# Seven-product weight sums of the second MLP formed in the streaming buffer, with the elementwise sums on VectorE

## The chip, the cores and the metric

The kernel runs on one core of one Trainium2 chip. The metric is the device time of one execution in microseconds (us). TensorE multiplies matrices, VectorE, ScalarE and GpSimd work elementwise, and SyncE (SP) issues nearly all transfers; each engine runs its own stream of instructions in order and waits for the others by semaphores.

## The reference

Three stages follow each other: a causal attention with a bias from cumulated gates (4 batches, 8 heads, 576 positions, head size 64), a first MLP with a softmax and a layer norm (512 to 1024 to 512), and the second MLP, which the change is in:

```
def _moe2_ref(x, w_in, w_out):        # x: 2304 x 512, w_in: 512 x 2048, w_out: 2048 x 512
    h = x @ w_in
    relu6 = np.clip(h + 3.0, 0.0, 6.0)
    g = h * relu6 / 6.0
    return (g @ w_out).astype(np.float32)
```

The weights come in 64-bit floats and are decoded on the chip. Each 32-bit factor is kept as a high and a low part, and each product is three matmuls: high by high, low by high, high by low.

## The kernel before

A planner (`Plan`, L51) sets the order. The functions call `plan.add(engine, cost, function, reads, writes, ...)`, and `emit` runs a greedy list schedule by the costs written there; what it gives is one fixed stream for each engine. `lag` is the planner's guess of how long a transfer takes to land, `new` names a ring of buffers, `bank` asks for one of eight PSUM banks.

The second MLP treats its 2304 tokens in groups of three tiles of 128 rows, so 384 tokens in one matmul. The hidden 2048 units are 16 blocks of 128 (`m`), or 8 pairs (`k`).

*The first six tiles* are two trios (`ci` 0 and 1), computed directly. For a trio and a block, `ffn2_h` does twelve matmuls (L1120: x parts `xk` by weight parts `wp`) into a bank; `gated` takes the bank through ScalarE (relu, L1097), VectorE (multiplication, L1100, tile `ggs`), ScalarE (high part, L1104) and VectorE (low part, L1107, tile `gs`); `ffn2_out` does nine matmuls (L1132: `gs` by `w2o`) into three accumulator banks. Trio 1 runs 3.5 blocks behind trio 0 (`DELAY`), and output matmuls come two items after their product (`LAG`). Beside these items the weights of the later blocks are decoded by `split64`: a raw load on SP (L321, L323; 512 KB each, in a ring of two buffers and one single buffer), ScalarE's shift (L329), VectorE's unit extraction (L333) and join (L337), the high part on ScalarE (L346), the low part on VectorE for the input weights and on GpSimd for the output weights (both L353).

*The last twelve tiles* are two batches (`bi`) of six tiles. For a pair of hidden blocks, a product of 2x2 blocks is done with seven block products in place of eight (`pair_h`: 42 matmuls, L1272, from x forms `xb` and weight forms `ws`; sums of the products `c` on VectorE, L1285), then four gates and 36 output matmuls. Six banks hold the six tiles' accumulators. The x forms come from `load_x2_pair`: four loads `xs` (L1205) into the places of trio 0's x parts, the split on ScalarE (L1212) and VectorE (L1215), and four differences `less` on GpSimd (L1218).

*The weight forms* are made ahead, beside the first six tiles, and kept in DRAM (`ws_d`). For a pair, `pair_parts` stores three pieces of the decoded weights as they are (L1153, L1157; 256 KB each). `pair_sums` makes a full sum of the weights' two parts (L1166, 1024 elements a partition), four sums of quarters (L1171 to L1174), a high part on ScalarE (L1178), a low part on VectorE (L1181), and stores both (L1184; 512 KB each). The sums of pairs 0 to 3 are on GpSimd, those of pairs 4 to 7 on VectorE (`SUMS_DVE`). `load_pair` then loads all seven forms of a pair in one transfer of 1792 KB (L1248) into a ring of two buffers, for either batch; these buffers take the place that the raw buffers had.

## Time and profile before

| | us |
|---|---|
| median of three runs (844.49 to 845.88) | 844.82 |
| the profiled execution, whole | 844.44 |
| its span, first to last instruction | 842.6 |
| TensorE busy | 805.1 |
| VectorE busy | 544.1 |
| ScalarE busy | 422.6 |
| GpSimd busy | 254.6 |

The granted TensorE clock was 0.994 of full speed over the span. The second MLP's direct six tiles lie at about 445 to 585 us, the two batches of six tiles behind them to the end. Busy times are sums over stages of different kinds; a timeline of one engine gives for each group of instructions its start, its length, and in brackets how long the engine idled before it and what ended that.

### The profile page before, as it was taken

What the parts mean: (1) busy time and instruction counts of PE and PEld (TensorE: products, weight loads), DVE (VectorE), ACT (ScalarE), POOL (GpSimd) and SP (SyncE); (2) the same over time, 40 slices, a digit from 0 to 9 for tenths busy, and PEclk for the clock granted to TensorE, in tenths of its full rate; (3) what the DMA queues carried; (4) which work ended last, traced back from release to release, by engine and by line L of the source; (5) the groups of instructions that cost most, each with busy time, mean ns of one, the idle gap of its engine ahead of it and who ended that gap; (6) DMA issues with size and microseconds to landing.
All of it is one profiled execution on the core that took longest, in us unless ns stands there. A gap on an engine that the chain in (4) does not pass through costs nothing.

```text
span 842.6 us, 14160 instructions
## 1 busy us (share of the span) xinstructions
PE 805.1 (96%) x4960; PEld 698.2 (83%) x4960; DVE 544.1 (65%) x1300; ACT 422.6 (50%) x986; POOL 254.6 (30%) x336
## 2 busy tenths in 40 slices
PE   3889999999999999999999988998999999999998
PEld 2655588898898889888998977997999898898896
DVE  3687887746855574749727999767645457555451
ACT  2575768755765575737535564334423234423223
POOL 2464644424633363327305564004000000000000
PEclk9999999999999999999999999999999999999999
DMA  6753596755555455233505566968522422623302
GB/s 160 191 154 110 120 221 144 176 122 126 129 119 135 103 124 120 65 110 115 189 32 159 198 214 228 306 201 287 213 87 98 165 88 100 237 89 109 154 1 75
DMA packets 113670, 121.60 MB, mean 144 GB/s; under 512 B 65120, under 2 KB 95328, under 8 KB 111552
## 3 DMA queue, kind: packets, MB, share of 16 engines
q1 hardware_dynamic: 111296, 112.32, 46.4%
q10 hardware_dynamic: 2304, 8.39, 3.0%
q8 instruction: 39, 0.64, 0.3%
q14 instruction: 31, 0.25, 0.1%
HBM read 74.74 MB, written 24.71 MB: 118 GB/s over the span
## 4 chain that ended last, share of the span: by engine, by line
PE 80%; DVE 11%; DMA 4%; issue 2%; POOL 2%; ACT 1%; SPq 0%; DVEq 0%; POOLq 0%; ACTq 0%
PE bank L1132 19%; PE bank L1272 14%; PE bank L905 11%; PE bank L818 10%; PE bank L713 6%; PE bank L616 5%; PE bank L684 5%; PE bank L1120 4%; PE bank L589 3%; PE bank L884 2%; DVE gs L1107 2%; DVE wp L353 2%; PE bank L479 1%; DVE t_w2i L333 1%; DVE a_w2o L337 1%
## 5 line engine op out<-in xcount | busy, mean ns | idle before, releaser
L1132 PE MATMUL bank<-w2o,gb 128*128 128x512 f32 x576 | 136.4, 391 | 0.0
L1132 PEld LDWEIGHTS bank<-w2o,gb 128*128 128x128 f32 x576 | 107.7, 188 | 21.0
L1272 PE MATMUL bank<-xb,ws 128*128 128x384 f32 x672 | 122.7, 336 | 0.6 <-DVE c L1285 0.6
L1272 PEld LDWEIGHTS bank<-xb,ws 128*128 128x128 f32 x672 | 118.3, 188 | 3.5 <-DVE c L1285 1.0
L1285 DVE TENSOR_TENSOR c<-c,bank 128x384 f32<-128x384 f32 x112 | 60.3, 552 | 83.7 <-PE bank L1272 70.0
L537 DVE CUSTOM_DVE_ANT_0 y<-bank,mask 96x288 f32<-96x288 f32 (+4 forms) x168 | 74.6, 467 | 57.2 <-PE bank L616 38.2
L549 ACT ACTIVATE y<-y,nmax 128x256 f32<-128x256 f32 (+4 forms) x140 | 83.5, 598 | 40.7 <-DVE nmax L537 28.4
L632 POOL TENSOR_SCALAR y<-y,rsum 128x128 f32<-128x128 f32 (+4 forms) x120 | 68.3, 588 | 103.4 <-DVE rsum L628 42.6
L905 PE MATMUL bank<-zh,w_out_h 128*128 128x256 f32 x288 | 82.9, 288 | 0.0
L905 PE MATMUL bank<-zh,w_out_l 128*128 128x256 f32 x288 | 81.0, 281 | 0.0
L905 PE MATMUL bank<-zl,w_out_h 128*128 128x256 f32 x288 | 81.0, 281 | 0.0
L1120 PE MATMUL bank<-xk,wp 128*128 128x384 f32 x384 | 74.8, 343 | 6.2 <-DVE ggs L1100 4.2
L1132 PE MATMUL bank<-w2o,gs 128*128 128x512 f32 x288 | 74.4, 403 | 3.6 <-DVE gs L1107 3.6
L1120 PEld LDWEIGHTS bank<-xk,wp 128*128 128x128 f32 x384 | 68.6, 191 | 11.1 <-DVE ggs L1100 6.2
L1132 PEld LDWEIGHTS bank<-w2o,gs 128*128 128x128 f32 x288 | 54.8, 193 | 14.7 <-DVE gs L1107 4.9
L1218 POOL TENSOR_TENSOR xs<-xs,xs 128x768 f32<-128x768 f32 x8 | 16.6, 2069 | 157.4 <-DVE xb L1215 112.6
L1097 ACT ACTIVATE ggb<-c 128x384 f32<-128x384 f32 x64 | 32.3, 522 | 58.2 <-DVE c L1285 57.6
L818 PE MATMUL bank<-w_in_h,xh 128*128 128x512 f32 x144 | 60.7, 421 | 0.8 <-DVE xh L800 0.8
L616 PE MATMUL bank<-stack 128*96 128x288 f32 (+4 forms) x288 | 57.9, 318 | 0.6 <-DMA stack<-rows_d 0.6
L818 PE MATMUL bank<-w_in_h,xl 128*128 128x512 f32 x144 | 56.8, 394 | 0.6 <-POOL xl L804 0.6
L818 PE MATMUL bank<-w_in_l,xh 128*128 128x512 f32 x144 | 56.7, 394 | 0.0
L905 PEld LDWEIGHTS bank<-zh,w_out_h 128*128 128x128 f32 x288 | 54.3, 189 | 1.1 <-DVE zl L891 0.2
(241 smaller groups left out, 1572.1 us busy)
## 6 DMA issues: line engine op xcount, KB each, us to landing
ws<-ws_d SPq DMA_DIRECT2D x16, 1792.0 KB
raw_w2i<-in_moe_w_in_dram SPq DMA_DIRECT2D x16, 512.0 KB
...
```

Of the source, the lines that this page charges most:

```text
L537: nc.vector.tensor_tensor_reduce(out=ys[h, t][:n, c0:c1], in0=bank(key)[:n, : c1 - c0], in1=mask[:n, 480 + n - w + c0 : 480 + n - w + c1], ...
L549: nc.scalar.activation(out=y[:n], in_=y[:n], func=AF.Exp, bias=nmax[:n, h, t : t + 1], scale=-1.0, accum_out=sums[:n, h, t : t + 1])
L616: nc.tensor.matmul(bank(key)[:n, : c1 - c0], lhsT=ss[:, 2 - 2 * m, ST[t] : w], rhs=ss[:, 3 - 2 * m, c0:c1], start=(m == 0), stop=(m == 1))
L632: nc.gpsimd.tensor_scalar(ys[h, t][:n], ys[h, t][:n], rsum[:n, h, t : t + 1], 1.0, ALU.mult, ALU.mult)
L684: nc.tensor.transpose(bank(key)[: SZ[jj], c : c + SZ[t]], ys[h, t][: SZ[t], ST[jj] : ST[jj] + SZ[jj]], ident[: SZ[t], : SZ[t]])
L713: nc.tensor.matmul(bank(key)[j * D : (j + 1) * D, lo - c0 : c1 - c0], lhsT=vs[v_key(p, a)][:n, jj, j, :], rhs=pts[pt_key(2 * p + j, a)][:n ...
L818: nc.tensor.matmul(bank(key), lhsT=xs[i][m // 2][:, kk, :], rhs=(w_in_l if m == 1 else w_in_h)[:, kk, f * 512 : (f + 1) * 512], start=(kk ...
L905: nc.tensor.matmul(bank(key)[:, : 2 * P], lhsT=w_out_at(w, kk)[:, m * P : (m + 1) * P], rhs=z[:, kk, :], start=(kk == 0 and i == 0), stop= ...
L1120: nc.tensor.matmul(bank(key)[:, :W], lhsT=w2p[m // 2][:, a, m % 2, c * P : (c + 1) * P], rhs=x[:, b, :], start=(c == 0 and i == 0), stop=( ...
L1132: nc.tensor.matmul(bank(key), lhsT=g_t[name][:, i // 2, (t % TRIO) * P : (t % TRIO + 1) * P], rhs=w2o[m][:, i % 2, :], start=(m == 0 and i ...
L1272: nc.tensor.matmul(bank(key)[:, :W], lhsT=ws[bi, k][:, WOP[op], x, kc * P : (kc + 1) * P], rhs=xb[bi, op][:, y, kc, :], start=(kc == 0 and ...
L1285: nc.vector.tensor_add(g_t[to_key], g_t[from_key], bank(key)[:, :W])
```

## The change

The decoded input weights of a pair, so far one tile `wp` of four pieces, become a tile `wp` of three pieces and a tile `wq` of one. All four pieces of all eight pairs are stored to `ws_d` as they are, in 32 stores of 256 KB, ordered behind the last raw load (`PAIRS_AT`, `after=`). The two `dec` pools close when all weights are decoded, and the ring `ws` opens in their place, now during the first six tiles. For the first batch, a load brings only the four pieces of a pair (1 MB); VectorE makes the full sums into tiles `tail` (in the places of `wq0` and `wq1`), the quarter sums there, ScalarE and VectorE write the high and low parts of the three further forms into the same `ws` buffer, and two stores keep them in `ws_d`. The second batch loads all seven forms of a pair as before. The sums of pairs 0 and 1 stand beside the direct items of the first six tiles, those of pairs 2 to 7 one pair ahead in the first batch. The four differences of a batch (`less`) move from GpSimd to VectorE.

```diff
-SUMS_BEHIND = 3
-SUMS_DVE = 4
+PAIRS_AT = 11
...
-            w2p[k] = pools[home_of(m)].tile([P, 2, 2, 512], F32R, tag=f"wp{k}", name=f"wp{k}")
+            w2p[k] = pools[home_of(m)].tile([P, 3, 512], F32R, tag=f"wp{k}", name=f"wp{k}"), pools[home_of(m)].tile([P, 512], F32R, tag=f"wq{k}", name=f"wq{k}")
...
     def pair_parts(k):
         key = f"wsd{k}"
...
-        for x in range(2):
-            plan.add("SP", 0.5, lambda x=x: store(x), reads=w2i_keys(2 * k), writes=[f"{key}/{x}"], lag=5.0, after=[f"wsd{k // 2 + 2}/3"])
-        plan.add("SP", 0.5, lambda: nc.sync.dma_start(out=ws_d[k, :, 2, :, :], in_=w2p[k][:, :, 1, 2 * P :].bitcast(F32)), ...)
+        def store(o, x):
+            nc.sync.dma_start(out=ws_d[k, :, 2 * o : 2 * o + 2, x, :], in_=w2i_at(2 * k + o, x).rearrange("p (o f) -> p o f", o=2).bitcast(F32))
+
+        for o in range(2):
+            for x in range(2):
+                plan.add("SP", 0.5, lambda o=o, x=x: store(o, x), reads=w2i_keys(2 * k + o), writes=[f"{key}/{2 * o + x}"], lag=4.0, after=[f"raw_w2o{KFF2 - 1}"])

     def pair_sums(k):
...
-        eng, name, us = (nc.gpsimd, "POOL", pool_tt) if k < SUMS_DVE else (nc.vector, "DVE", dve)
...
-        plan.add(name, us(1024), full, reads=w2i_keys(2 * k) + w2i_keys(2 * k + 1) + ["last"], writes=[f], new=[("full", 1, f)])
-        plan.add(name, 4 * us(256), sums, reads=[f], writes=[sk], new=[("sm", 1, sk)])
-        plan.add("ACT", act(1024), high, reads=[sk], writes=[f])
-        plan.add("SP", 0.5, lambda: store_sums(0, "h"), reads=[f], writes=[f"{key}/3"], lag=5.0)
-        plan.add("DVE", dve(1024), low, reads=[f], writes=[sk])
-        plan.add("SP", 0.5, lambda: store_sums(1, "s"), reads=[sk], writes=[f"{key}/4"], lag=5.0)
+        def full(i):
+            T[i] = pools["w2a"].tile([P, 2, 2 * P], F32, tag=f"wq{i}", name=t[i])
+            w = ws[0, k][:, 2 * i : 2 * i + 2]
+            nc.vector.tensor_add(T[i], w[:, :, 0, :].bitcast(F32), w[:, :, 1, :].bitcast(F32))
...
+        for i in range(2):
+            plan.add("DVE", dve(512), lambda i=i: full(i), reads=[f"{key}/a"], writes=[t[i]], new=[(f"wq{i}", 1, t[i])])
+        plan.add("DVE", 4 * dve(256), sums, reads=[f"{key}/a"], writes=t)
+        for i in (1, 0):
+            plan.add("ACT", act(512), lambda i=i: nc.scalar.copy(of(i, 0), T[i]), reads=[t[i], f"{key}/a"], writes=[f"{key}/h{i}"])
+            plan.add("DVE", dve(512), lambda i=i: nc.vector.tensor_sub(of(i, 1), T[i], of(i, 0).bitcast(F32)), reads=[t[i], f"{key}/h{i}"], writes=[f"{key}/l{i}"])
+        for i, o in ((1, slice(5, 7)), (0, slice(2, 5, 2))):
+            plan.add("SP", 0.5, lambda o=o: nc.sync.dma_start(out=ws_d[k, :, o], in_=ws[0, k][:, o].bitcast(F32)), reads=[f"{key}/{x}{i}" for x in "hl"], writes=[f"wsd{k}/s{i}"], lag=4.0)
...
-            plan.add("POOL", pool_tt(2 * W), lambda: nc.gpsimd.tensor_sub(raw_x[bi, to], raw_x[bi, a], raw_x[bi, b]), ...)
+            plan.add("DVE", dve(2 * W), lambda: nc.vector.tensor_sub(raw_x[bi, to], raw_x[bi, a], raw_x[bi, b]), ...)
...
-                     new=[(f"xk0{i}", 1, key(i))], lag=4.0)
+                     new=[(f"xk0{i}", 1, key(i))], lag=6.0)
...
-    WOP = {0: 0, 1: 1, 2: 4, 4: 3, 5: 5, 3: 2, 6: 6}
+    WOP = {0: 0, 1: 1, 2: 2, 3: 3, 6: 4, 5: 5, 4: 6}
...
-            nc.sync.dma_start(out=ws[bi, k].bitcast(F32), in_=ws_d[k])
+            if bi:
+                nc.sync.dma_start(out=ws[bi, k].bitcast(F32), in_=ws_d[k])
+            else:
+                nc.sync.dma_start(out=ws[bi, k][:, 0:4].bitcast(F32), in_=ws_d[k, :, 0:4])
...
-        if ci and 2 * summed + 1 + SUMS_BEHIND <= m:
-            pair_sums(summed)
-            summed += 1
-        if (ci, m) == (0, KFF2 - 1):
-            while summed < KFF2 // 2:
-                pair_sums(summed)
-                summed += 1
+        if (ci, m) == (1, PAIRS_AT):
             for k in range(KFF2 // 2):
                 pair_parts(k)
...
             for k in range(2):
                 load_pair(0, k)
+                pair_sums(k)
+        if (ci, m) == (0, KFF2 - 1):
+            load_x2_pair(0)
...
             pair_h(bi, k)
+            if not bi and 1 < k + 1 < KFF2 // 2:
+                pair_sums(k + 1)
```

What stands in a row on the engines is shown at three places. In the names, `wp0` to `wp7` and `wq0` to `wq7` are the weight tiles of pairs 0 to 7, `full` and `s` the sums of before, `tail0` and `tail1` those of after for pairs 0 and 1 (the second number is the half), `ggs1_8` the gate of trio 1 and block 8, `gs1_8` its parts.

On SyncE, around the last raw load, before:

```order
L321 DMA raw_w2i15_5736<-in_moe2_w_in_dram 128x4x256
L1184 DMA ws_d_106<-full2_5647 128x4x256
L1184 DMA ws_d_106<-s2_5687 128x4x256
L1153 DMA ws_d_106<-wp0_4427 128x2x256 x2
L1157 DMA ws_d_106<-wp0_4427 128x2x256
L1153 DMA ws_d_106<-wp1_4428 128x2x256 x2
L323 DMA raw_w2o15_5794<-in_moe2_w_out_dram 128x1024
L1157 DMA ws_d_106<-wp1_4428 128x2x256
L1184 DMA ws_d_106<-full3_5817 128x4x256
L1153 DMA ws_d_106<-wp2_5239 128x2x256 x2
L1184 DMA ws_d_106<-s3_5856 128x4x256
```

After (the stores of `wp0` to `wp5` and the raw load `raw_w2o15` stand straight ahead of these, with no other row between):

```order
L1155 DMA ws_d_106<-wq5_5259 128x2x256
L1155 DMA ws_d_106<-wp6_5260 128x2x256 x3
L1155 DMA ws_d_106<-wq6_5261 128x2x256
L1155 DMA ws_d_106<-wp7_5262 128x2x256 x3
L1155 DMA ws_d_106<-wq7_5263 128x2x256
L1246 DMA ws0_0_5905<-ws_d_106 128x2048
L1246 DMA ws0_1_5913<-ws_d_106 128x2048
L1187 DMA ws_d_106<-ws0_0_5905 128x1024
L1187 DMA ws_d_106<-ws0_0_5905 128x2x512
L1187 DMA ws_d_106<-ws0_1_5913 128x1024
```

Before, stores of parts and of sums alternate, and the whole-pair loads come much later, behind the x loads; after, the stores are one train, and the loads of four pieces and the stores of two pairs' sums stand right behind it, ahead of the x loads `xs0`.

On VectorE, around the gate of block 11 of trio 0, before:

```order
L1171 TENSOR_TENSOR s4_5954<-full4_5939 128x256
L1172 TENSOR_TENSOR s4_5954<-s4_5954,full4_5939 128x256
L1173 TENSOR_TENSOR s4_5954<-full4_5939 128x256
L1174 TENSOR_TENSOR s4_5954<-full4_5939,s4_5954 128x256
L1100 SCALAR_TENSOR_TENSOR ggs0_11_5961<-ggs0_11_5961,bank3_94 128x384
L1181 TENSOR_TENSOR s4_5954<-s4_5954,full4_5939 128x1024
L1107 TENSOR_TENSOR gs0_11_5975<-ggs0_11_5961,gs0_11_5975 128x384
L1100 SCALAR_TENSOR_TENSOR ggs1_8_5994<-ggs1_8_5994,bank6_97 128x384
L1107 TENSOR_TENSOR gs1_8_6006<-ggs1_8_5994,gs1_8_6006 128x384
L1166 TENSOR_TENSOR full5_6023<-wp5_5258 128x1024
```

After:

```order
L1102 SCALAR_TENSOR_TENSOR ggs0_11_5947<-ggs0_11_5947,bank3_94 128x384
L1171 TENSOR_TENSOR tail0_0_5954<-ws0_0_5905 128x512
L1171 TENSOR_TENSOR tail0_1_5961<-ws0_0_5905 128x512
L1109 TENSOR_TENSOR gs0_11_5958<-ggs0_11_5947,gs0_11_5958 128x384
L1175 TENSOR_TENSOR tail0_1_5961<-tail0_1_5961 128x256
L1176 TENSOR_TENSOR tail0_1_5961<-tail0_0_5954,tail0_1_5961 128x256
L1177 TENSOR_TENSOR tail0_0_5954<-tail0_1_5961,tail0_0_5954 128x256
L1178 TENSOR_TENSOR tail0_0_5954<-tail0_0_5954 128x256
L1102 SCALAR_TENSOR_TENSOR ggs1_8_5982<-ggs1_8_5982,bank6_97 128x384
L1185 TENSOR_TENSOR ws0_0_5905<-tail0_1_5961,ws0_0_5905 128x2x256
L1185 TENSOR_TENSOR ws0_0_5905<-tail0_0_5954,ws0_0_5905 128x2x256
```

Before, a sum there is of a pair's decoded weights in place; after, the first sum reads the buffer `ws0_0` that the load on SyncE fills, and the low part of block 11 and the gate of block 8 of trio 1 stand behind it.

On VectorE, at the passage from the direct items to the batches, from the multiplication of block 12 of trio 1 to its low part, before:

```order
L1100 SCALAR_TENSOR_TENSOR ggs1_12_6260<-ggs1_12_6260,bank6_97 128x384
L1215 TENSOR_TENSOR xb0_0_6272<-xs0_0_6212,xb0_0_6272 128x768
L1215 TENSOR_TENSOR xb0_1_6280<-xs0_1_6217,xb0_1_6280 128x768
L1100 SCALAR_TENSOR_TENSOR ggs1_13_6296<-ggs1_13_6296,bank3_94 128x384
L1215 TENSOR_TENSOR xb0_6_6299<-xs0_3_6254,xb0_6_6299 128x768
L1215 TENSOR_TENSOR xb0_4_6308<-xs0_0_6212,xb0_4_6308 128x768
L1215 TENSOR_TENSOR xb0_5_6327<-xs0_2_6234,xb0_5_6327 128x768
L1107 TENSOR_TENSOR gs1_12_6334<-ggs1_12_6260,gs1_12_6334 128x384
L1107 TENSOR_TENSOR gs1_13_6340<-ggs1_13_6296,gs1_13_6340 128x384
```

After:

```order
L1210 TENSOR_TENSOR xb0_0_6236<-xs0_0_6183,xb0_0_6236 128x768
L1213 TENSOR_TENSOR xs0_0_6183<-xs0_2_6196,xs0_0_6183 128x768
L1213 TENSOR_TENSOR xs0_2_6196<-xs0_3_6204,xs0_2_6196 128x768
L1210 TENSOR_TENSOR xb0_1_6243<-xs0_1_6188,xb0_1_6243 128x768
L1210 TENSOR_TENSOR xb0_6_6255<-xs0_3_6204,xb0_6_6255 128x768
L1213 TENSOR_TENSOR xs0_3_6204<-xs0_3_6204,xs0_0_6183 128x768
L1213 TENSOR_TENSOR xs0_1_6188<-xs0_1_6188,xs0_3_6204 128x768
L1210 TENSOR_TENSOR xb0_4_6261<-xs0_0_6183,xb0_4_6261 128x768
L1210 TENSOR_TENSOR xb0_2_6296<-xs0_3_6204,xb0_2_6296 128x768
L1210 TENSOR_TENSOR xb0_5_6272<-xs0_2_6196,xb0_5_6272 128x768
L1210 TENSOR_TENSOR xb0_3_6307<-xs0_1_6188,xb0_3_6307 128x768
L1109 TENSOR_TENSOR gs1_12_6280<-ggs1_12_6217,gs1_12_6280 128x384
```

Before, five splits and one more gate stand between the two; after, seven splits and the four differences. On TensorE, the product of block 15 of trio 1 and the products `ws0_0` by `xb0_0` and by `xb0_1` now stand between the output matmuls of block 12 of trio 1 that read the high part and those that read the low part; before, all nine output matmuls of that block stood together.

## Rows read from the trace of the kernel before

**Rows 1.** The page's chain of work that ended last, by engine.

```profile
PE 80%; DVE 11%; DMA 4%; issue 2%; POOL 2%; ACT 1%; SPq 0%; DVEq 0%; POOLq 0%; ACTq 0%
```

**Rows 2.** Timeline of TensorE, 556 to 585: start us, us, engine line op, tiles, count [idle, releaser].

```profile
571.14 2.27 PE L1120 MATMUL bank<-xk,wp 128*128 128x384 f32 x12
573.25 0.63 PE L1132 MATMUL bank<-w2o,gs 128*128 128x512 f32 x2
577.17 3.36 PE L1132 MATMUL bank<-w2o,gs 128*128 128x512 f32 x7 [3.30 <-DVE gs L1107]
580.33 2.39 PE L1120 MATMUL bank<-xk,wp 128*128 128x384 f32 x12
```

**Rows 3.** The same view, 446 to 461.

```profile
450.10 2.24 PE L1132 MATMUL bank<-w2o,gs 128*128 128x512 f32 x9
452.18 1.23 PE L1120 MATMUL bank<-xk,wp 128*128 128x384 f32 x6
...
456.30 0.62 PE L1120 MATMUL bank<-xk,wp 128*128 128x384 f32 x2 [1.50 <-ACT xk L1079]
...
459.92 1.41 PE L1120 MATMUL bank<-xk,wp 128*128 128x384 f32 x4
```

**Rows 4.** Timeline of GpSimd, 446 to 461.

```profile
447.69 2.40 POOL L1166 TENSOR_TENSOR full<-wp 128x1024 f32<-128x1024 f32 x1 [23.53 <-DVE ggs L1100]
...
460.26 1.36 POOL L353 TENSOR_TENSOR w2o<-a_w2o,w2o 128x512 fp32r<-128x512 f32 x1 [1.28 <-ACT w2o L346]
```

**Rows 5.** Timeline of VectorE, 446 to 461.

```profile
447.77 2.74 DVE L1107 TENSOR_TENSOR gs<-ggs,gs 128x384 fp32r<-128x384 f32 x1 [0.58 <-ACT gs L1104]
...
455.73 0.69 DVE L337 SCALAR_TENSOR_TENSOR a_w2o<-a_w2o,t_w2o 128x512 int32<-128x512 int32 x1
456.34 0.55 DVE L1107 TENSOR_TENSOR gs<-ggs,gs 128x384 fp32r<-128x384 f32 x1
```

**Rows 6.** Timeline of TensorE, 495 to 526.

```profile
496.05 2.25 PE L1132 MATMUL bank<-w2o,gs 128*128 128x512 f32 x9
...
515.21 2.35 PE L1120 MATMUL bank<-xk,wp 128*128 128x384 f32 x12 [1.47 <-DVE ggs L1100]
...
525.10 1.11 PE L1120 MATMUL bank<-xk,wp 128*128 128x384 f32 x5
```

**Rows 7.** Busy time by stretch (us): length, engines (x count), TensorE's clock, DMA share, GB/s.

```profile
480.00:520.00 40.00, 36.12 (x175) 30.88 (x173) 39.48 (x49) 22.70 (x42) 23.76 (x19) 1.00 0.70 233
520.00:530.00 10.00, 9.39 (x47) 8.23 (x47) 7.20 (x12) 4.38 (x8) 2.19 (x2) 1.00 0.62 205
534.00:540.00 6.00, 6.00 (x33) 5.61 (x32) 4.30 (x9) 1.91 (x4) 0.00 (x0) 1.00 1.04 343
```

**Rows 8.** VectorE's groups, 460 to 530: line, op, tiles, count | busy us, mean ns | idle.

```profile
L1107 DVE TENSOR_TENSOR gs<-ggs,gs 128x384 fp32r<-128x384 f32 x15 | 13.1, 876 | 0.6 <-ACT gs L1104 0.6
L353 DVE TENSOR_TENSOR wp<-a_w2i,wp 128x512 fp32r<-128x512 f32 x10 | 11.9, 1192 | 0.0
L337 DVE SCALAR_TENSOR_TENSOR a_w2i<-a_w2i,t_w2i 128x512 int32<-128x512 int32 x10 | 11.3, 1129 | 0.7
```

**Rows 9.** Timeline of VectorE, 556 to 585.

```profile
569.78 5.26 DVE L1215 TENSOR_TENSOR xb<-xs,xb 128x768 fp32r<-128x768 f32 x3 [1.49 <-ACT xb L1212]
```

**Rows 10.** Timeline of TensorE, 690 to 700.

```profile
696.28 2.36 PE L1272 MATMUL bank<-xb,ws 128*128 128x384 f32 x12 [0.65 <-DVE c L1285]
```

**Rows 11.** Timeline of SyncE's queue, 397 to 404.

```profile
398.24 0.38 SPq L321 DMA_DIRECT2D raw_w2i<-in_moe_w_in_dram  x1
```

**Rows 12.** Timeline of VectorE, 397 to 404.

```profile
402.49 1.37 DVE L333 TENSOR_SCALAR t_w2i<-raw_w2i 128x512 int32<-128x512 uint32 x1 [1.18 <-DMA raw_w2i<-in_moe_w_in_dram]
```

**Rows 13.** Groups of all engines, 520 to 580 (columns as in rows 8).

```profile
L1166 DVE TENSOR_TENSOR full<-wp 128x1024 f32<-128x1024 f32 x4 | 4.9, 1220 | 0.0
...
L1171 DVE TENSOR_TENSOR s<-full 128x256 f32<-128x256 f32 x4 | 1.7, 424 | 2.1 <-DMA ws_d<-s 2.1
```

**Rows 14.** VectorE's groups, 590 to 690.

```profile
L1285 DVE TENSOR_TENSOR c<-c,bank 128x384 f32<-128x384 f32 x46 | 24.7, 552 | 35.6 <-PE bank L1272 30.0 <-ACT c L1287 4.2 <-DVE c L1285 0.5
```

More of the change, by code (lines that the diff above doesn't have):

```diff
@@ L1027, in last_pools @@
             pools[name] = ctx.enter_context(tc.tile_pool(name=name, bufs=1, side="right"))
-        for name in ("dec3", "sb"):
-            pools[name] = tops_ctx.enter_context(tc.tile_pool(name=name, bufs=1, side="right"))
+        pools["dec3"] = tops_ctx.enter_context(tc.tile_pool(name="dec3", bufs=1, side="right"))
     def pair_pools():
@@ L1150, in pair_parts @@
         key = f"wsd{k}"
-        def store(x):
-            nc.sync.dma_start(out=ws_d[k, :, 0:2, x, :], in_=w2p[k][:, x, 0, :].rearrange("p (o f) -> p o f", o=2).bitcast(F32))
-        for x in range(2):
-            plan.add("SP", 0.5, lambda x=x: store(x), reads=w2i_keys(2 * k), writes=[f"{key}/{x}"], lag=5.0, after=[f"wsd{k // 2 + 2}/3"])
-        plan.add("SP", 0.5, lambda: nc.sync.dma_start(out=ws_d[k, :, 2, :, :], in_=w2p[k][:, :, 1, 2 * P :].bitcast(F32)), reads=w2i_keys(2 * k + 1), writes=[f"{key}/2"], lag=5.0, after=[f"wsd{k // 2 + 2}/3"])
+        def store(o, x):
+            nc.sync.dma_start(out=ws_d[k, :, 2 * o : 2 * o + 2, x, :], in_=w2i_at(2 * k + o, x).rearrange("p (o f) -> p o f", o=2).bitcast(F32))
@@ L1159, in pair_sums @@
+        for o in range(2):
+            for x in range(2):
+                plan.add("SP", 0.5, lambda o=o, x=x: store(o, x), reads=w2i_keys(2 * k + o), writes=[f"{key}/{2 * o + x}"], lag=4.0, after=[f"raw_w2o{KFF2 - 1}"])
     def pair_sums(k):
+        key, t = f"ws0_{k}", [f"tail{k}_{i}" for i in range(2)]
         T = {}
-        eng, name, us = (nc.gpsimd, "POOL", pool_tt) if k < SUMS_DVE else (nc.vector, "DVE", dve)
-        def full():
-            T["full"] = pools["sb"].tile([P, 2, 512], F32, tag="full", name=f"full{k}")
-            eng.tensor_add(T["full"], w2p[k][:, 0].bitcast(F32), w2p[k][:, 1].bitcast(F32))
@@ L1168, in sums @@
-        def sums():
-            T["s"] = sm = pools["sb"].tile([P, 4, 2 * P], F32, tag="s", name=f"s{k}")
-            (a11, a12), (a21, a22) = ((T["full"][:, i, : 2 * P], T["full"][:, i, 2 * P :]) for i in range(2))
-            eng.tensor_add(sm[:, 0], a21, a22)
-            eng.tensor_sub(sm[:, 1], sm[:, 0], a11)
-            eng.tensor_sub(sm[:, 2], a11, a21)
-            eng.tensor_sub(sm[:, 3], a12, sm[:, 1])
-        def high():
-            T["h"] = T["full"].rearrange("p i (o f) -> p (i o) f", o=2)
-            nc.scalar.copy(T["h"].bitcast(F32R), T["s"])
@@ L1180, in low @@
-        def low():
-            nc.vector.tensor_sub(T["s"].bitcast(F32R), T["s"], T["h"])
-        def store_sums(x, src):
-            nc.sync.dma_start(out=ws_d[k, :, 3:7, x, :], in_=T[src])
-        f, sk, key = f"full{k}", f"sm{k}", f"wsd{k}"
-        plan.add(name, us(1024), full, reads=w2i_keys(2 * k) + w2i_keys(2 * k + 1) + ["last"], writes=[f], new=[("full", 1, f)])
-        plan.add(name, 4 * us(256), sums, reads=[f], writes=[sk], new=[("sm", 1, sk)])
-        plan.add("ACT", act(1024), high, reads=[sk], writes=[f])
@@ L1247, in load @@
             ws[bi, k] = pools["ws"].tile([P, 7, 2, 2 * P], F32R, tag="ws", name=key)
-            nc.sync.dma_start(out=ws[bi, k].bitcast(F32), in_=ws_d[k])
-        plan.add("SP", 1.0, load, reads=["pairs", *(f"wsd{k}/{x}" for x in range(5))], writes=[key], new=[("ws", 2, key)], lag=9.0)
+            if bi:
+                nc.sync.dma_start(out=ws[bi, k].bitcast(F32), in_=ws_d[k])
+            else:
+                nc.sync.dma_start(out=ws[bi, k][:, 0:4].bitcast(F32), in_=ws_d[k, :, 0:4])
+        plan.add("SP", 1.0, load, reads=["pairs", *(f"wsd{k}/{x}" for x in ([*range(4), "s0", "s1"] if bi else range(4)))], writes=[f"{key}/a"], new=[("ws", 2, key)], lag=8.0 if bi else 6.0)
     def pair_h(bi, k):
@@ L1273, in mm @@
                                          start=(kc == 0 and i == 0), stop=(kc == 1 and i == 2))
-            plan.add("PE", 6 * pe(W) + 0.01, mm, reads=[f"ws{tag}", f"xb{bi}_{op}/h", f"xb{bi}_{op}/l"], writes=[key], bank=key)
+            plan.add("PE", 6 * pe(W) + 0.01, mm, reads=[f"ws{tag}/a", *([] if bi else [f"ws{tag}/{x}{i}" for x in "hl" for i in range(2)]), f"xb{bi}_{op}/h", f"xb{bi}_{op}/l"], writes=[key], bank=key)
         def sum_of(to, name, op):
@@ L1337 @@
     late = []
-    summed = 0
     for ci, m in items:
```

20 lines of the change are left out of this document (14 added, 6 removed).

## The prediction

> **What bounds the kernel now.** The chain that ended last is read first: 80% of it is TensorE and 11% VectorE [rows 1]. TensorE is the bound, so a change can only win where TensorE stands still or is slowed; the rest of the reading looks for those places in TensorE's timeline of the second MLP. The pitch is the measure: twelve product matmuls of an item take 2.11 us (571.14 to 573.25, [rows 2]) and its nine output matmuls 2.08 us (450.10 to 452.18, [rows 3]), so an item costs 4.19 us, one row of 128 hidden units (both trios) 8.37 us, and a start that comes later than its predecessors' pitches allow is lost time. Three places lose:
>
> - Beside the first sum of GpSimd. From 450.10 to 459.92 TensorE runs 9 + 12 + 9 matmuls, 6.27 us of work, in 9.82 us: 3.55 us lost, ended by x high and low parts [rows 3]. GpSimd's full sum of 2.40 us starts at 447.69 [rows 4], and a gate's low part on VectorE that starts beside it takes 2.74 us where the same line takes 0.55 later [rows 5]. That late VectorE made the x parts late.
> - The stretch of weight decoding. From 496.05 to 525.10 there are six output items and five products, 23.0 us of work in 29.05 us: 6.05 us lost, in waits for a gate on VectorE of which the longest is shown [rows 6]. VectorE is busy 39.48 of 40 us there [rows 7]. Its groups say why: the gate's low part averages 876 ns, a weight's low part 1192 ns and the join of an input weight 1129 ns [rows 8], where the same gate line takes 0.55 undisturbed and a join 0.69 [rows 5], which I also take for the weight's low part of as many elements.
> - The passage to the last twelve tiles. Two matmuls start at 573.25 and the other seven of that item only at 577.17, after 3.30 us of idling for a gate's low part on VectorE, and they take 3.36 us [rows 2]; the next start comes at 580.33, 7.08 us after 573.25 where 2.08 was due: 5.0 us. VectorE's three splits before that low part took 5.26 us [rows 9], beside differences on GpSimd.
>
> A fourth, small one is at the change of batch: 0.65 us for a sum on VectorE [rows 10]. The sum of all is 15.3 us.
>
> **The change part by part.** *Sums leave GpSimd.* All twenty GpSimd sum instructions and the eight differences go. What stays on GpSimd in the decoding stretch is the output weights' low part, one of 1.36 us per row [rows 4]. VectorE's own work per row is then two gates' multiplications and two low parts (4 x 0.55) and two unit extractions, two joins and a low part (at most 5 x 0.69): 5.7 us; with the whole 1.36 us of the remaining GpSimd instruction lost to it, 7.0 of 8.37 us. It is no longer bound, so I take the first two losses as gone: -3.55 and -6.05. Bounds: nothing back of the second if the disturbance is not the sums (0), all of it if it is; I take all, since the three groups alone are stretched by 15 x 0.33 + 10 x 0.50 + 10 x 0.44 = 14.3 us in 70 us, and the some eight low parts on GpSimd in that time make up only 11 us, if every one held VectorE for its whole length.
>
> *Stores and the new load.* 24 stores of 256 KB, spread among the 16 of 512 KB with the sums, become 32 of 256 KB in one train, 8.39 MB, directly behind the last raw load (the sums' own stores follow pair by pair, later); behind them on the same queue stands the first load for the sums (1.05 MB). I count from t = 0, the end of the product of block 8 of the first trio. The last raw load is issued when the unit extraction of block 14 is done, about +1.1. Raw load, stores and load are 0.52 + 8.39 + 1.05 = 9.96 MB. The rate is that of the 6 us in which the kernel before stores without a gap (its 256 and 512 KB stores, the same 1 KB pieces): 343 GB/s [rows 7], so 29.0 us. To that comes the time of issue and of the last completion: a 512 KB load was issued at 398.24 and released VectorE at 402.49 [rows 11, 12], 4.25 us for 1.5 us of bytes with others in flight, so between 0 and 2.7; I take 1.5. The load lands at +31.6 (30.1 to 32.8).
>
> VectorE meets the first sum in order right behind the gate of block 11 of trio 0, which is done at about +26.2 (3 x 8.37 and two gate operations), and stands there some 5 us. Queued behind it: the low part of that gate, the gate of block 8 of trio 1, the second pair's sums and the gate of block 12 of trio 0. From the landing to the end of that last gate VectorE has 2 x 0.61 + 0.55 + 4 x 0.42 + 0.55 + 2 x 0.61 + 0.55 and again 2 x 0.61 + 1.7 + 0.55, 9.2 us with the pitch a little under the durations (a full sum or a low part of 1024 is 1.22, a quarter sum 0.42, [rows 13]). TensorE wants the bank that this gate frees for block 13: 4 x 8.37 to the end of block 12's product, then 2.08 + 2.11 + 2.08, +39.7. The loss is landing + 9.2 - 39.7, so 1.1 us (0 to 2.3). The two earlier needs (the low part at +34.0, the bank of block 8 at +35.6) are met. Each microsecond of later landing costs one more.
>
> A rule of the Trainium skill speaks against this part: "SBUF — State Buffer", section "The DMA setup-cost knee", gives each transfer some 2 us that do not depend on its size, beside bytes at 436 GB/s. By it a store of 256 KB is 2.6 us, 32 in single file 83 us, the landing near +92 and the time near 891. The 343 GB/s above, with several stores outstanding, says that these fixed parts overlap here; what is left of the rule stands as a chance among the slow stores below.
>
> *The passage.* The differences go to VectorE, so eleven operations of about 0.93 (768 elements, between the 0.55 of 384 and the 1.22 of 1024) stand between block 12's multiplication of trio 1 and its low part, 10.2 us, where before it were five plus GpSimd. But they are undisturbed, no stores of sums stand between the four x loads any more, and TensorE's order now puts the product of block 15 and the first two block products (2.1 us) between the passes that need only the high part and the one that needs the low. Walked so, the x loads start at the end of block 15's product of trio 0 (+2.1 from its start), land 4 to 6 us later, the low part is there at about +17 and wanted at about +20. I take the 5.0 us as gone; bounds 0 and 5.
>
> *The first batch.* Seven sums and eight gate operations of 0.55 [rows 14] are 8.3 us of VectorE per pair; the tail adds 1.22 + 1.7 + 1.22, 12.5 in all, of a pair of 42 x 0.175 + 36 x 0.231 = 15.7 us. It fits in sum; in order the tightest place is the sixth sum, whose bank comes free some 0.4 us before TensorE wants it. I take no cost; a miss costs 0 to 2 us per pair, six times. The load of each pair is issued when its buffer is free and lands about 3 us before VectorE comes to it; loads shrink from 1.8 to 1.05 MB while the sums' stores come beside them, hidden under the same 15.7 us. The copies on ScalarE (two of 512 for one of 1024) add little to an engine that isn't in the chain. TensorE's matmuls stay the same in number and size; the cut of a weight tile into three quarters and one changes addresses, and the planner's longer lag for the x loads only the order: nothing for both.
>
> *The change of batch.* The order of the products moves; I take 0.5 of the 0.65 us.
>
> Sum, against the profiled execution's own 844.44 us (span 842.6; the median of the runs, 844.82, is 0.4 above it): 844.44 - 3.55 - 6.05 - 5.0 - 0.5 + 1.1 = 830.4; I say 830.5.
>
> **The rivals.** (a) *The stores decide.* The load lands late and VectorE, standing at the sum, keeps gates from TensorE. For it: the stretch 520 to 530, half stores, moves only 205 GB/s [rows 7]. At that rate the 9.96 MB take 48.6 us, the landing is +51.2, the loss 20.7 and the time 850: slower. It costs all gains from a landing of +45.6 on, when the train runs at 231 GB/s. Against it: in 520 to 530 the queue waited for sums; in 534 to 540 it did not. Milder forms (landing +33 to +40) give 832 to 839. (b) *VectorE becomes the bound of the first batch*: six pairs lose 1 to 2 us each, 836.5 to 842.5. For it: 12.5 of 15.7 us in a fixed order with six banks held by accumulators. Against it: nothing on GpSimd stretches it now. (c) *The passage keeps its gap*: eleven operations in a row on VectorE; the 5 us stay, 835.5. (d) *The change doesn't free VectorE*: GpSimd's remaining low parts disturb it enough to keep the 6 us; 836.5.
>
> **How the numbers follow.** The forecast (829 to 833) has 0.56; (a) mild 0.08, near no change 0.03 and slower 0.05; (b) 0.13, (c) 0.09, (d) 0.06. The low end is the loss at its lower bound and the whole 0.65 of the batch change, 829.2, and a little for scatter: 828.5. Leaving out (a) slow, the upper half of (b) and the worst mild cases, the top is 840. Faster by over 0.2% (1.7 us, about what a measurement of this kernel tells from no change) 0.92, within it 0.03, slower 0.05.
>
> **What would show it.** Right: VectorE under 80% busy in the decoding stretch, its lines at 0.55 and 0.69; no wait of TensorE there; the stores moving some 340 GB/s without a gap; one wait of VectorE for the first load of about 5 us, and after it at most 2 us of TensorE idle; no 3 us wait at the passage; TensorE at pitch through the first batch. Wrong: TensorE waiting on gates for long right after the wait for the load (a), on sums in each pair (b), on a low part before the first products (c), or a stretched VectorE beside GpSimd's low parts (d).

## The result, and the profile after

The changed kernel takes 831.67 us (median of four runs between 831.4 and 833.97); the kernel before took 844.65 beside it. The ratio is 0.9854 with an interval of 0.9829 to 0.9879: 13 us faster, where 830.5 (828.5 to 840.0) was forecast. The profiled execution took 831.66 us with a span of 829.9, so 12.7 us of span are gone. Line numbers shift a little: L1100, L1107, L1120, L1132, L1272 and L1285 of before are L1102, L1109, L1122, L1134, L1270 and L1283 after.

The page's chain of work, by engine, answers to [rows 1]. VectorE's 11% have become 4%:

```profile
PE 89%; DVE 4%; DMA 4%; POOL 2%; issue 1%; ACT 1%; SPq 0%; POOLq 0%; DVEq 0%; ACTq 0%
```

These are all the waits that TensorE has left from 395 us to the end, so in the second MLP (who waited for whom, us in total, times, longest):

```profile
PE bank L1122 <- DVE ggs L1102: 1.0, 2, 0.7
PE bank L1134 <- DVE gs L1109: 1.0, 1, 1.0
```

*The decoding stretch.* Busy time by stretch, columns as in [rows 7]:

```profile
460.00:480.00 20.00, 20.00 (x103) 18.21 (x102) 18.72 (x33) 14.46 (x28) 3.95 (x3) 1.00 0.71 230
480.00:520.00 40.00, 40.00 (x202) 36.16 (x201) 25.79 (x42) 19.82 (x38) 8.56 (x6) 1.00 0.91 298
493.00:519.00 26.00, 26.00 (x132) 23.47 (x131) 13.56 (x23) 10.63 (x21) 4.01 (x3) 1.00 1.04 343
494.00:495.00 1.00, 1.00 (x7) 0.96 (x7) 1.00 (x2) 0.83 (x2) 1.00 (x1) 1.00 0.86 144
495.00:496.00 1.00, 1.00 (x8) 1.00 (x7) 1.00 (x2) 0.23 (x1) 0.33 (x1) 1.00 0.92 225
```

In 480 to 520 TensorE is busy 40.00 of 40 us (36.12 before) and VectorE 25.79 (39.48 before). VectorE's 25.79 is a mean over two things: while it decodes VectorE is still busy 18.72 of 20 us (460 to 480), and the last low part of an input weight ends at 502.4 (520.3 before), so that the rest of the stretch has gates alone. VectorE's groups of 460 to 490, all within the decoding, to lay beside [rows 8] (count | busy us, mean ns):

```profile
L336 DVE SCALAR_TENSOR_TENSOR a_w2i<-a_w2i,t_w2i 128x512 int32<-128x512 int32 x7 | 6.8, 965 | 0.4
...
L1109 DVE TENSOR_TENSOR gs<-ggs,gs 128x384 fp32r<-128x384 f32 x8 | 4.4, 547 | 0.0
...
L352 DVE TENSOR_TENSOR wp<-a_w2i,wp 128x512 fp32r<-128x512 f32 x4 | 3.7, 928 | 0.1
...
L352 DVE TENSOR_TENSOR wq<-a_w2i,wp 128x512 fp32r<-128x512 f32 x3 | 2.0, 679 | 0.0
```

The gate's low part takes 547 ns, its undisturbed time (in [rows 8], which go to 530, 876). The others are helped less: a weight's low part has 928 (`wp`) and 679 (`wq`), over 460 to 530 some 780 in the mean of both instead of 1192, and a join of an input weight 965, over 460 to 530 903 instead of 1129. The long ones stand beside the output weights' low parts, which GpSimd keeps: joins of 1.66 and 1.67 us start at 465.09 and 469.66, GpSimd's instructions of 1.29 us at 464.92 and 469.49. There is no wait of TensorE where [rows 3] and [rows 6] had theirs.

*The train of stores and the load behind it.* SyncE's queue: the last two raw loads, and the two loads of four pieces behind the 32 stores:

```profile
491.17 0.38 SPq L320 DMA_DIRECT2D raw_w2i<-in_moe_w_in_dram  x1
493.18 0.33 SPq L322 DMA_DIRECT2D raw_w2o<-in_moe_w_out_dram  x1
...
518.92 1.36 SPq L1246 DMA_DIRECT2D ws<-ws_d  x2
```

VectorE at the first sum (timeline; the bracket is its idle time before):

```profile
517.88 0.56 DVE L1102 SCALAR_TENSOR_TENSOR ggs<-ggs,bank 128x384 f32<-128x384 f32 x1 [2.49 <-ACT ggs L1099]
525.29 1.29 DVE L1171 TENSOR_TENSOR tail<-ws 128x512 f32<-128x512 f32 x2 [6.85 <-DMA ws<-ws_d]
```

TensorE beside it:

```profile
525.48 0.63 PE L1134 MATMUL bank<-w2o,gs 128*128 128x512 f32 x2
527.11 1.89 PE L1134 MATMUL bank<-w2o,gs 128*128 128x512 f32 x7 [1.00 <-DVE gs L1109]
529.29 0.44 PE L1122 MATMUL bank<-xk,wp 128*128 128x384 f32 x1 [0.29 <-DVE ggs L1102]
...
534.47 0.45 PE L1122 MATMUL bank<-xk,wp 128*128 128x384 f32 x1 [0.72 <-DVE ggs L1102]
...
536.66 2.24 PE L1134 MATMUL bank<-w2o,gs 128*128 128x512 f32 x9
```

The load lands 32.1 us after the issue of the last raw load, VectorE has stood 6.85 us, and TensorE, which at 525.48 begins two outputs and two products of 8.37 us, begins the next only at 536.66: 2.8 us lost in three waits of 1.00, 0.29 and 0.72 us and the starts behind them.

*The passage.* TensorE and VectorE where [rows 2] and [rows 9] were:

```profile
565.90 1.55 PE L1134 MATMUL bank<-w2o,gs 128*128 128x512 f32 x6
...
569.38 2.24 PE L1270 MATMUL bank<-xb,ws 128*128 128x384 f32 x12
571.46 0.86 PE L1134 MATMUL bank<-w2o,gs 128*128 128x512 f32 x3
```

```profile
564.04 3.56 DVE L1210 TENSOR_TENSOR xb<-xs,xb 128x768 fp32r<-128x768 f32 x4
567.52 0.55 DVE L1109 TENSOR_TENSOR gs<-ggs,gs 128x384 fp32r<-128x384 f32 x1
```

TensorE starts each group as the last one ends. Block 12's low part is begun at 567.52 and is ready before TensorE, which first does other products, comes to it at 571.46.

So 3.55 + 6.05 + 5.0 + 0.65 us are regained and 2.8 lost, 12.45; the spans differ by 12.7.

### The profile page after: what moved, and what is told of

It reads as the page before. It is cut to its first block, busy times and chain, and to the rows that moved or that the text cites. A ratio compares the mean times of both kernels' runs of the same rounds, so it can differ in the third digit from the quotient of the medians.

```text
span 829.9 us, 14168 instructions
## 1 busy us (share of the span) xinstructions
PE 800.3 (96%) x4960; PEld 696.4 (84%) x4960; DVE 539.0 (65%) x1344; ACT 423.6 (51%) x994; POOL 209.2 (25%) x308
## 4 chain that ended last, share of the span: by engine, by line
PE 89%; DVE 4%; DMA 4%; POOL 2%; issue 1%; ACT 1%; SPq 0%; POOLq 0%; DVEq 0%; ACTq 0%
PE bank L1134 23%; PE bank L1270 14%; PE bank L904 11%; PE bank L817 11%; PE bank L1122 7%; PE bank L712 6%; PE bank L615 5%; PE bank L683 5%; PE bank L588 3%; PE bank L883 2%; PE bank L478 1%; DMA ws<-ws_d 1%; POOL y L649 1%; DMA rows_d<-neg 1%; DMA whole<-rows_d 1%
## 5 line engine op out<-in xcount | busy, mean ns | idle before, releaser
L1134 PE MATMUL bank<-w2o,gb 128*128 128x512 f32 x576 | 137.2, 391 | 0.0
L1134 PEld LDWEIGHTS bank<-w2o,gb 128*128 128x128 f32 x576 | 107.6, 188 | 20.9
L1270 PE MATMUL bank<-xb,ws 128*128 128x384 f32 x672 | 123.5, 336 | 0.0
L1270 PEld LDWEIGHTS bank<-xb,ws 128*128 128x128 f32 x672 | 118.5, 188 | 2.9
L1283 DVE TENSOR_TENSOR c<-c,bank 128x384 f32<-128x384 f32 x112 | 60.4, 551 | 63.6 <-PE bank L1270 60.1
L1122 PE MATMUL bank<-xk,wp 128*128 128x384 f32 x320 | 72.2, 338 | 1.0 <-DVE ggs L1102 1.0
L1134 PE MATMUL bank<-w2o,gs 128*128 128x512 f32 x288 | 72.0, 393 | 1.0 <-DVE gs L1109 1.0
L1134 PEld LDWEIGHTS bank<-w2o,gs 128*128 128x128 f32 x288 | 53.5, 188 | 11.0 <-DVE gs L1109 1.4
L1122 PEld LDWEIGHTS bank<-xk,wp 128*128 128x128 f32 x320 | 57.3, 188 | 3.7 <-DVE ggs L1102 1.9
L683 PE MATMUL bank<-ident,y 128*128 128x128 f32 (+2 forms) x420 | 51.5, 258 | 3.2 <-POOL y L649 2.3
```

The costliest lines, as they stand in the source:

```text
L683: nc.tensor.transpose(bank(key)[: SZ[jj], c : c + SZ[t]], ys[h, t][: SZ[t], ST[jj] : ST[jj] + SZ[jj]], ident[: SZ[t], : SZ[t]])
L1122: nc.tensor.matmul(bank(key)[:, :W], lhsT=w2i_at(m, a)[:, c * P : (c + 1) * P], rhs=x[:, b, :], start=(c == 0 and i == 0), stop=(c == KDM ...
L1134: nc.tensor.matmul(bank(key), lhsT=g_t[name][:, i // 2, (t % TRIO) * P : (t % TRIO + 1) * P], rhs=w2o[m][:, i % 2, :], start=(m == 0 and i ...
L1270: nc.tensor.matmul(bank(key)[:, :W], lhsT=ws[bi, k][:, WOP[op], x, kc * P : (kc + 1) * P], rhs=xb[bi, op][:, y, kc, :], start=(kc == 0 and ...
L1283: nc.vector.tensor_add(g_t[to_key], g_t[from_key], bank(key)[:, :W])
```

## The experiments

Nine more kernels were run. The changed kernel itself was run once more beside the first three of them:

> The changed kernel once more, beside the others on the same chip. Expected 831.7 us, with the one cluster of TensorE waits of the second MLP (1.00, 0.29 and 0.72 us behind VectorE's wait for the first load of four pieces) in the same place.

It took 831.92 us (ratio 0.9847, 0.9833 to 0.9862); its load landed 32.3 us after the last raw load's issue, and TensorE waited 2.2 us in the same place.

### The sums of the first two pairs later on VectorE

```diff
-        ..., lag=8.0 if bi else 6.0)
+        ..., lag=8.0 if bi else 14.0 if k < 2 else 6.0)
```

> The planner is told that the first two loads take 14 us instead of 6, which moves the sums of pairs 0 and 1 on VectorE behind two more gates and leaves everything else in place. Theory (what is left of TensorE's idling is VectorE standing at the sum while the load is under way): the wait of VectorE falls from 6.9 to about 1.6 us and costs nothing, TensorE has no wait left in the second MLP, and the time falls by the 2.7 us that the changed kernel loses there, to 829.0. Rival (the sums' own work on VectorE, twice 4.3 us beside the gates, is what TensorE waits for): the waits only move, 831 to 832.

Measured: 828.86 us, ratio 0.9812 (0.9797 to 0.9827). TensorE has no wait after 395 us. VectorE still waits for the load, 1.74 us in place of 6.85, with nothing urgent queued behind it:

```profile
525.11 0.69 DVE L1171 TENSOR_TENSOR tail<-ws 128x512 f32<-128x512 f32 x1 [1.74 <-DMA ws<-ws_d]
```

So the loss behind the load is where VectorE stands in its order, not the work of the sums. This is the fastest kernel of all that were run: one planner's guess, 3 us better than the change.

### The two loads in the other order

The two buffers are still taken in the old order, ahead of the loads (those lines are not shown):

```diff
+            for k in (1, 0):
                 load_pair(0, k)
+            for k in range(2):
                 pair_sums(k)
```

> The two loads of four pieces are issued in the other order, pair 1 ahead of pair 0; VectorE's order stays but for the gate of block 12, which comes some 1.7 us earlier in it. Theory (transfers of one queue that are outstanding together share the rate, so the first to be issued lands nearly when both are through): the load of pair 0 lands at most 1 us later than in the changed kernel, 33 to 34 us after the end of block 8's product, and the time stays within 830.5 to 832.5. Rival (first issued, first landed): it lands 3 us later, at +36, and the time goes to 833 to 835.

Measured: 834.68 us, ratio 0.9884 (0.9862 to 0.9905); the load of pair 0 lands at 529.0, 34.7 us after the last raw load's issue against 32.1 and 32.3:

```profile
529.00 0.69 DVE L1171 TENSOR_TENSOR tail<-ws 128x512 f32<-128x512 f32 x1 [9.42 <-DMA ws<-ws_d]
```

It comes 2.4 to 2.6 us later, not under 1, so the theory of a shared rate falls in that form: what is issued first lands first, nearly by its whole 3 us. Beside that there is a time between the last bytes and the landing. Busy time by stretch shows that the transfers of both loads have all but ended by 527, two microseconds before the second one is told to have landed (GB/s is the last column). At the 397 GB/s of the first row the 1.05 MB of one load take 2.6 us, so two loads one after the other, each with the same time behind its last byte, would give the measured difference; that is an estimate, and what the two microseconds are stays open:

```profile
525.00:527.00 2.00, 2.00 (x13) 1.81 (x11) 0.00 (x0) 0.00 (x0) 0.00 (x0) 1.00 0.96 397
527.00:530.00 3.00, 0.25 (x2) 0.00 (x0) 0.99 (x2) 0.00 (x0) 0.00 (x0) 1.00 0.05 22
...
533.00:536.00 3.00, 2.88 (x9) 2.88 (x10) 2.97 (x6) 1.42 (x3) 0.00 (x0) 0.50 0.50 192
```

The same rows show a cost that the wait alone doesn't have: TensorE idled from 527 to 530, and the granted clock is 0.50 in 533 to 536. The profiled execution, 836.96 us, is the slowest of the four, so its loss is larger than the median's 3 us.

### Eight more stores ahead of the load

```diff
+            for n in range(8):
+                plan.add("SP", 0.0, lambda n=n: nc.sync.dma_start(out=more_d[n], in_=w2i_at(n, 0)...), ..., after=[f"raw_w2o{KFF2 - 1}"])
```

> Eight more stores of 256 KB into a scratch tensor stand behind the 32, ahead of the first load; the planner gives them no cost, so every engine's order stays. Theory (the train of stores sets when the sums can begin, and each microsecond of it beyond +30.5 is one of TensorE's): 2.1 MB at 343 GB/s are 6.1 us, the load lands at about +39 and the time is 837.8. Rival (the loss behind the load is not the train's): within 1 us of the changed kernel, 832.

Measured: 837.71 us, ratio 0.9915 (0.9896 to 0.9933), 5.8 us above the changed kernel beside it (831.92). The load lands 38.1 us after the last raw load's issue, 6.0 later, and TensorE's wait for block 11's low part is one of 7.89:

```profile
531.55 1.29 DVE L1172 TENSOR_TENSOR tail<-ws 128x512 f32<-128x512 f32 x2 [13.74 <-DMA ws<-ws_d]
```

```profile
533.37 3.35 PE L1135 MATMUL bank<-w2o,gs 128*128 128x512 f32 x7 [7.89 <-DVE gs L1110]
```

The train sets the time of the first sum: 6.0 us more of it are 5.8 us of time. The seven matmuls behind the wait take 3.35 us where 1.89 was usual.

### The differences back on GpSimd

```diff
-            plan.add("DVE", dve(2 * W), lambda: nc.vector.tensor_sub(raw_x[bi, to], ...
+            plan.add("POOL", pool_tt(2 * W), lambda: nc.gpsimd.tensor_sub(raw_x[bi, to], ...
```

> The changed kernel with the four differences of a batch back on GpSimd; the planner then puts TensorE's and VectorE's order at the passage back to that of the kernel before, too. Theory A (the gap of 5 us at the passage came from GpSimd's differences, which stretch VectorE's splits beside them): a gap of 3 to 5 us before an output matmul of block 12 is back, 835 to 837. Theory B (it came from x loads that landed late, because stores of sums stood between them): the loads are issued together at about 552 and the last lands near 557; with the 8.3 us that the kernel before took from there to the low part, the low part is ready at 565.5, when TensorE comes to it: gap under 1 us, 831.5 to 832.7.

Measured: 835.7 us, ratio 0.99 (0.9872 to 0.9927), 4.0 above the changed kernel (3.2 in the profiled executions, 834.86 and 831.66). The x loads came early, as theory B has it, and still there is a gap, of 2.0 us (with 0.7 more at the change of batch). GpSimd's differences and VectorE's splits beside them:

```profile
558.30 4.20 POOL L1213 TENSOR_TENSOR xs<-xs,xs 128x768 f32<-128x768 f32 x2 [52.61 <-DMA xs<-x_d]
```

```profile
561.17 2.14 DVE L1210 TENSOR_TENSOR xb<-xs,xb 128x768 fp32r<-128x768 f32 x1 [0.17 <-ACT xb L1207]
```

```profile
568.56 1.88 PE L1134 MATMUL bank<-w2o,gs 128*128 128x512 f32 x7 [1.98 <-DVE gs L1109]
```

A split of 0.95 us takes 2.14 beside a difference. Neither theory alone holds: with the early loads some 3 of the 5 us stay away, and the differences, with the old order that goes with them, make the rest. Differences and order weren't taken apart.

### The kernel before with all sums on VectorE

```diff
-SUMS_DVE = 4
+SUMS_DVE = 0
```

> The kernel before with the sums of all eight pairs on VectorE. It adds 4.2 us of work to VectorE for each of four pairs, and by the planner's order the last pair's sums and their stores move into the passage, between the splits. Theory (GpSimd's sums disturb VectorE by more than they save it): the first loss (3.55 us near 455) is under 1 us, that of the decoding stretch falls from 6 to 1 to 3 us though VectorE has more to do, the passage gets longer by 2 to 4 us; together 839 to 842. Rival (VectorE was bound by its own work there): the decoding stretch loses 6 us or more, 846 to 852.

Measured: 842.85 us, ratio 0.998 (0.9965 to 0.9995). VectorE has four pairs' sums more to do and is busy less, 33.11 of 40 us instead of 39.48, with the gate's low part at 614 ns and the weight's at 683:

```profile
480.00:520.00 40.00, 39.86 (x199) 35.63 (x198) 33.11 (x54) 21.24 (x39) 7.70 (x5) 1.00 0.67 216
```

```profile
L1107 DVE TENSOR_TENSOR gs<-ggs,gs 128x384 fp32r<-128x384 f32 x17 | 10.4, 614 | 0.0
...
L353 DVE TENSOR_TENSOR wp<-a_w2i,wp 128x512 fp32r<-128x512 f32 x10 | 6.8, 683 | 0.0
```

TensorE's waits from 395 us on:

```profile
PE bank L1132 <- ACT gs L1104: 6.1, 1, 6.1
...
PE bank L1272 <- ACT obacc L1137: 1.5, 1, 1.5
...
PE bank L1132 <- DVE gs L1107: 0.2, 1, 0.2
```

The 0.2 us is the only wait left where the first two losses were. By the pitch, the measure that gave 9.6 us before, 0.9 us is left: 6.30 us for the 6.27 of work from 450.37 on, and 30.18 for 29.33 from 496.45 on. Most of the gain is given back at the passage, where the planner now puts the last pair's sum and its stores: the two waits on ScalarE, 6.1 and 1.5 us, and some more, about 7 us in all by the spans (840.9 against 842.6) where 2 to 4 were expected. So the sums on GpSimd were the cause of the first two losses, and moving them to another engine isn't enough.

### The full sums on GpSimd made twice

```diff
+            for _ in range(2 if k < SUMS_DVE else 1):
                 eng.tensor_add(T["full"], w2p[k][:, 0].bitcast(F32), w2p[k][:, 1].bitcast(F32))
```

> The kernel before with the full sum of pairs 0 to 3 made twice in a row on GpSimd, so four more instructions of about 2.4 us on an engine that is idle there. Theory (VectorE's operations with both inputs in SBUF are held up for as long as GpSimd's sum runs): the first loss grows by about 2 us and each of the three sums in the decoding stretch costs 1 to 2.4 us more; 849 to 854. Rival (no such hold-up; VectorE is slow there for another reason): 844 to 846.

Measured: 854.41 us, ratio 1.0118 (1.0086 to 1.015), 9.8 us more for four instructions of 2.6 us on an engine off the chain. The waits for gates, 4.2 and 3.6 us by the same view of the kernel before, are longer:

```profile
PE bank L1120 <- DVE ggs L1100: 6.6, 6, 1.6
PE bank L1132 <- DVE gs L1107: 6.3, 3, 3.8
```

By the pitch the first two losses are 5.8 and 12.8 us here; the passage is 1.7 us longer as well. With the run before this one the dose runs both ways: no sum on GpSimd 0.9 us, each full sum once 9.6, twice 18.6 us.

### The kernel before with the differences on VectorE

```diff
-            plan.add("POOL", pool_tt(2 * W), lambda: nc.gpsimd.tensor_sub(raw_x[bi, to], ...
+            plan.add("DVE", dve(2 * W), lambda: nc.vector.tensor_sub(raw_x[bi, to], ...
```

> The kernel before with only the four differences of a batch on VectorE; TensorE's and VectorE's order at the passage become those of the changed kernel, the stores of sums still stand between the x loads. Theory A (GpSimd's differences make the gap): the gap falls from 5 us to under 1, 839.5 to 840.5. Theory B (the late x loads make it): the last load lands where it did, near 569, eight operations of 0.95 stand behind it on VectorE, and TensorE's new order asks for the low part at about 576.7 instead of 573.9; a gap of 0.5 to 2 us is left if nothing is stretched, and 3 or more only if the loads land later still.

Measured: 845.14 us, ratio 1.0004 (0.9992 to 1.0016): nothing. Block 12's low part is nearly in time (a wait of 0.20 us), but a third wait closes the passage. ScalarE stands 7.00 us at the copy of the third accumulator, whose output buffer is held by a store that stands behind the two loads of 1.8 MB; the high part of block 13 is queued behind that copy:

```profile
582.12 0.60 ACT L1137 ACTIVATE obacc<-bank 128x512 f32<-128x512 f32 x1 [7.00 <-DMA out_dram<-obacc]
```

```profile
583.55 3.91 PE L1132 MATMUL bank<-w2o,gs 128*128 128x512 f32 x9 [3.79 <-ACT gs L1104]
```

### The same, with the load of pair 1 behind the output stores

```diff
+            ..., after=["outacc2"] if (bi, k) == (0, 1) else ())
```

> The kernel before with the differences on VectorE (as in the run that did only that) and, in addition, the load of pair 1 (1.8 MB) issued behind the first three output stores instead of ahead of them; the engines' orders stay. Theory (in the old arrangement the passage is closed by a third wait: ScalarE's copy of the third accumulator waits for an output buffer whose store stands behind 3.7 MB of pair loads, 7.0 us, and behind that copy stands the high part that TensorE wants): the store lands some 5 us earlier, ScalarE is free at about 577, the gap of 3.8 us and TensorE's slow matmuls behind it go: 839 to 841. Rival (the splits on VectorE close the passage): within 1 us of that run, 844 to 846.

Measured: 842.52 us, ratio 0.9985 (0.9967 to 1.0002). ScalarE's wait is 1.81 us, and block 13's outputs start at 580.39 without one; but at 589.93 there is a new wait of 2.07, behind an x load of batch 1 that now stands behind the load of pair 1 (start, us, what; from the chain of waits):

```profile
577.73 0.60 ACT L1137 ACTIVATE obacc<-bank 128x512 f32<-128x512 f32 x1 [1.81 <-DMA out_dram<-obacc]
```

```profile
580.39 2.24 PE L1132 MATMUL bank<-w2o,gs 128*128 128x512 f32 x9
...
589.93 1.34 PE L1272 MATMUL bank<-xb,ws 128*128 128x384 f32 x6 [2.07 <-DVE c L1285]
```

```profile
579.26 8.63 DMA xs<-x_d
```

The 3.8 us went as the theory has it, but a wait of half that length came back one transfer further, and the time is above the 839 to 841 expected. In the old arrangement the stores of the last sums, the x loads of two batches, two loads of 1.8 MB and the output stores share the passage, and whichever is last is waited for.

### The sums back on GpSimd in the changed kernel

```diff
-            nc.vector.tensor_add(T[i], w[:, :, 0, :] ...      # and the four sums of quarters
+            nc.gpsimd.tensor_add(T[i], w[:, :, 0, :] ...
```

> The changed kernel with the full sums and quarter sums of all pairs on GpSimd; high and low parts stay where they are. VectorE no longer stands at a sum while the load is under way, but GpSimd works some 6 us per pair beside it in the first batch. Theory (a sum on GpSimd holds up VectorE's two-input operations for about its own length): the 2.7 us behind the load vanish or shrink, VectorE's means for sums and low parts in the first batch rise from 0.55 to 0.8 us and more, TensorE waits 1 to 3 us for each of six pairs: 835 to 847. Rival (GpSimd's sums do no harm where VectorE has room, 8.3 + 1.3 of 15.7 us): no waits in the batch, 829 to 830.

Measured: 831.69 us, ratio 0.985 (0.9826 to 0.9873), as the changed kernel. The theory falls for the batch: no wait there at all. The rival's 829 to 830 isn't reached either, for one wait is left behind the load:

```profile
PE bank L1122 <- DVE ggs L1102: 2.1, 1, 2.1
```

VectorE's sums of products and gates' low parts, 585 to 690, of this kernel, and the low parts of the changed one (count | busy us, mean ns):

```profile
L1283 DVE TENSOR_TENSOR c<-c,bank 128x384 f32<-128x384 f32 x45 | 24.3, 551 | 30.6 <-PE bank L1270 28.5 <-ACT c L1285 1.4
L1109 DVE TENSOR_TENSOR gb<-ggb,gb 128x384 fp32r<-128x384 f32 x26 | 15.6, 607 | 1.7 <-ACT gb L1106 0.6
```

```profile
L1109 DVE TENSOR_TENSOR gb<-ggb,gb 128x384 fp32r<-128x384 f32 x26 | 14.3, 554 | 1.4 <-ACT gb L1106 0.6
```

The low part, with both inputs in SBUF, takes 607 ns where it takes 554; the sum of products, with one input in a PSUM bank, stays at 551, its undisturbed time [rows 14].

## Why the prediction was right, point by point

*The first two losses* (-9.6) came back whole, and for the reason given: without GpSimd's sums VectorE does the same and more in less time (by the pitch, no sum on GpSimd: 0.9 us; the full sums twice: 18.6). The sign that was named for it, VectorE under 80% busy, did not come: it is 94% while it decodes (460 to 480) and 64% only in the mean of 480 to 520. The 5.7 us of work per 8.37 counted one decoded block of weights in that time, but the trace has nine joins of an input weight in 460 to 502, one in 4.7 us ([rows 8] has ten in 70 us already). VectorE fills the time that it gets with decoding ahead, and the gates come in time all the same.

*The train of stores* was sized at 1.1 us (0 to 2.3) and cost 2.8. The form of the term was right: loss = landing - 30.5 gives 2.6 for a landing at +33.1 (32.1 from the raw load's issue, which was at +1.0), and eight more stores cost 5.8 us of time for 6.0 us of landing. The two earlier needs, the low part and the bank of block 8, which were taken as met, are where TensorE waited first (1.00 and 0.29 us), as they must with a landing 1.5 us later. What was too small was the landing itself, taken at +31.6 and at most +32.8. The rate was not the step that failed: from the issue of the last raw load to the landing (493.18 to 525.29) the queue moved 346 GB/s in the mean, with the low 144 and 225 GB/s of 494 to 496 in it. What failed is the count of the bytes and the time behind them. The raw load issued at 491.17, two microseconds ahead, wasn't counted; in those two microseconds 0.18 MB moved (91 GB/s), so at least 0.34 of its 0.52 MB were still to come, 1.0 us. With them 10.3 MB stood ahead of the landing; that much had moved by 523.3 (341 GB/s over 30.1 us), and the landing is told 2.0 us later, where 1.5 were taken. The run with the loads in the other order shows such two microseconds with hardly any traffic (527 to 529.0). As the views don't tell one load's bytes from another's, this split is an estimate; its 1.0 and 0.5 us are the 1.5 that were missing. The price of the whole term could have been none, as the later sums show.

By the setup rule of the Trainium skill ("SBUF — State Buffer", section "The DMA setup-cost knee") in single file the load would have landed near +92, an estimate from the page's figures. The trace has +33.1, with 343 GB/s over the 26 us of the train (493 to 519): the fixed parts overlapped, and of the rival of slow stores only its mild form is in the result.

*The passage* gave the 5.0 us, but the reasons listed were not all. The prediction named the differences, the stores between the x loads and TensorE's new order. The differences off GpSimd alone gave nothing, because ScalarE was held by output stores queued behind 3.7 MB of pair loads; and with them on GpSimd in the changed kernel only 2.0 of the 5 us came back. The change also takes the pair loads out of the passage, 50 us ahead, and by the two runs of the kernel before that counts too; the prediction left it out of its sum, so that the full 5.0 us came in part by luck. No run puts the pair loads back into the passage of the changed kernel.

*The first batch* lost nothing, as taken: no wait of TensorE there, with VectorE's tail in it, and rival (b) didn't come. *The change of batch* lost none of its 0.65 us (0.5 was taken).

*Rival (d)*, that GpSimd's remaining low parts would keep VectorE from its gates, fell by its price, not by its sign: the input weights' join (965 ns) and low part (928 for `wp`) stay stretched and VectorE is busy 94% of the time while it decodes, but TensorE has no wait there. *Rival (a)* was the right one to fear: its mechanism is what is left of the loss.
